# A channel gate over an image that is larger than the on-chip memory: other chunk sizes, and GpSimd beside VectorE

## The chip, the cores and the metric

The kernel runs on one core of a Trainium2 chip. The metric is the device time of one execution in microseconds (us), as the median of several runs; lower is better. Engines are named as in the profile: PE is TensorE, DVE is VectorE, ACT is ScalarE, POOL is GpSimd, SP is the engine whose queue issues nearly all DMA transfers here.

## What is computed

```
H = W = 384; C = 384; k = 1
x: (1, H, W, C) bfloat16, w1d: (1,) bfloat16

g = einsum("bhwc->bc", x) / (H * W)      # mean of each channel
s = sigmoid(g * w1d[0])                  # k = 1: a kernel of one tap
return x * s[:, None, None, :]
```

The whole image has to be summed before the first output value is known. x has 147,456 pixels of 384 channels, 113.25 MB, and the output has as many.

## The kernel before

**Tiles and rows.** The pixels are split over the 128 partitions, 1152 per partition. The program calls one pixel per partition a row: 384 bf16 numbers (768 bytes) in each partition, 98,304 bytes over all. One large tile, the arena, holds 275 rows. Everything is loaded into it, changed in place, and stored from it.

**First phase: sum, and keep what fits.** All 1152 rows are loaded once. TensorE adds each row into a PSUM bank with a matrix of ones (`sum_rows`, one matmul per row, line 242). 784 rows are streamed: summed, overwritten, and read a second time later. The other 368 are kept. Of those, 72 raw rows stay as they are, and the rest sits in groups that are folded. A group of q row quadruples is loaded as 4q rows. `fold` (line 292) spreads the 16 bits of every fourth number over spare exponent bits of the three others, so that q of the 4q rows come free and the next group can be laid over them. There is one group with q = 4 (`FIRST`), eight with q = 8 (`PAIR`; 32 rows each, in two columns of the arena, at 12 and at G0 = 116), and one with q = 6 (`BANKED`) that ScalarE copies into PSUM and brings back later. A fold works in pieces of 16 rows (`PIECE` = 4 rows of each quarter), with scratch rows at T and Y. A vote (`seen`, `verdict`, `again`) has GpSimd redo the kept groups should a number not have the expected exponent; it doesn't with these inputs.

The order of the loads is written out by hand: after the first two groups the streamed rows go in chunks of 52 and of 64 (`EARLY`), then groups and chunks by turns (`BETWEEN`), the last three groups in parts because less of the arena is free, then the raw rows in small loads. On TensorE's queue the sums stand in the order of the loads. With chunks of over 40 rows 16 extra matmuls of a zero tile are put in front (`keep_warm`).

**The turn.** ScalarE makes the sigmoid (`s_bf`, line 451) and copies it into PSUM as well (`s_ps`, line 455).

**Second phase: scale and store.** `scale` (line 464) multiplies rows with the gate in place, on VectorE. Only at the start does GpSimd take three scales of 4 rows (`alongside`), while VectorE reads the gate from PSUM (`s_ps`) instead of SBUF (`s_bf`). `unfold` (line 484) rebuilds a piece of 16 rows in four steps: `fields`, `signs`, `three`, `fourth`. They are tensor_scalar operations on bits (line 276), joins (tensor_tensor, line 282) and scales. Stores (line 474) and the second loads of the streamed rows (line 236) go through SP's queue in order; an instruction at its head that waits holds up all behind it.

**The planner.** The order of the second phase comes from a small model that runs while the program is built (lines 576 to 781). It keeps a clock for VectorE and a list of transfers, and decides at each tick what is scaled, unfolded, stored or loaded next. Its output is an order of instructions, not times: on the chip only semaphores hold an instruction. Its parameters: VectorE prefers landed chunks to unfolding while less than `PENDING` us of transfers are ahead; scaled parts are stored together unless less than `MERGE` us are ahead; a load takes the longest free run of rows, up to `CAP`, if it has `BIG` rows, or less when under `LOW` or `LAST` us are ahead; a landed load is scaled in parts of at most `PART` rows; `DEEP` and `SHORT` say when a load may follow a store.

`Flow` (line 21) records every step with the rows it reads and writes and turns conflicts into semaphore waits. DMA completions use 24 semaphores per queue in turn.

Of the kernel before, what the change touches and what calls it, by code (L numbers as in the profile page):

```python
# [11 lines left out]
class Step:  # L12
    __slots__ = ("eng", "emit", "dma", "lane", "deps", "wanted", "rank", "waits", "know", "i")

    def __init__(self, eng, emit, dma):
        self.eng, self.emit, self.dma = eng, emit, dma
        self.deps, self.wanted, self.rank, self.waits, self.know = [], False, 0, [], None
        self.lane = None


class Flow:
# [12 lines left out]
    def add(self, eng, emit, reads=(), writes=(), dma=False, after=()):  # L34
        s = Step(eng, emit, dma)
        s.i = len(self.steps)
# [31 lines left out]
    def emit(self):  # L68
# [37 lines left out]
        with self.tc.tile_critical():  # L106
            for s in self.steps:
# [3 lines left out]
                for h, v in waits:  # L111
                    eng.wait_ge(h, v)  # L112
                ins = s.emit()
# [14 lines left out]
def kernel(  # L128
# [32 lines left out]
    N_A = 39  # L161
# [186 lines left out]
    folding = False  # L348
    N_WARM = 16

    def stream(n, a):
        load(STREAMED, a, streamed[0], streamed[0] + n)
        if n > 40 and folding:
            keep_warm(N_WARM)
        sum_rows(a, n)
        streamed[0] += n

    def stream_all(where, n=None):
        i = 0
        n = sum(m for _, m in where) if n is None else n  # L360
        while n:
            a, m = where[i % len(where)]
            m = min(n, m)
            stream(m, a)
            n -= m
            i += 1
# [30 lines left out]
    for i, (lo, hi, corner) in enumerate(corners):  # L397
        copy_bank(i, arena[:, SPARE, lo:hi], corner, rows(SPARE, 1), [("corner", i)])

    S1, S2 = [(A, 20)], [(A + 20, N_A - 20)]  # L400

    HIGH = [(A - 48, 48)]
    LOW_COLUMN = [(G0 - 48, 48)]


    take(FIRST)
    fold(0)
    EARLY = [(A - 64 * i, 64) for i in (3, 2, 1)]
    BETWEEN = [
        LOW_COLUMN, HIGH,  # L410
        LOW_COLUMN, [(A, N_A)],
        [(G0 - 24, 24), (A - 24, 24)], (S1, S2),
        (S1, S2), (S1, S2),
    ]
    between = sum(n for b in BETWEEN for w in b for _, n in (w if isinstance(w, list) else [w]))
    first = N_STREAM - between
    stream_all(EARLY[2:], first % 64)
    stream_all(EARLY, first - first % 64)
    folding = True


    for g, where in zip(range(1, BANKED), BETWEEN):
        k1, k2 = of_group(g)
        if isinstance(where, list):
            take(g)
            fold(k1)
            fold(k2)
            stream_all(where)
        else:
            take(g, 0, 12)  # L430
            take(g, 24, 32)
            fold(k1)
            stream_all(where[0])
            take(g, 12, 24)
            fold(k2)
            stream_all(where[1])
# [6 lines left out]
    for a, n in [(U, 8)] + S1 + [(A + 20, 11), (A + 31, 8), (V, 8), (Y + 1, 6), (T + 5, 4), (T + 2, 3), (T, 2)]:  # L443
        take_raw(a, n)
# [24 lines left out]

    def store(chunk, a, lo, hi):  # L470
# [7 lines left out]
    def unfold(k, first):  # L478

        g, lo, p = pieces[k]  # L480
        a, at = first + 3 * lo, first + 3 * GROUPS[g][1] + lo
        w, wc = flat(a, 3 * p), [rows(a + j * p, p) for j in range(3)]
        w0, w1, w2 = (flat(a + j * p, p) for j in range(3))
        ba, ca = Y, Y + PIECE
        u, b, c = flat(at, p), flat(ba, p), flat(ca, p)
        uc, bc, cc = rows(at, p), rows(ba, p), rows(ca, p)
        more = int(k == of_group(BANKED)[-1])

        def fields():
            bits(u, w0, SHR, 4, AND, 0x0780, wc[0], uc)  # L490
            bits(b, w1, SHR, 8, AND, 0x0078, wc[1], bc)
            join(u, u, b, OR, uc + bc, uc)

        def signs():
            bits(c, w2, SHR, 12, AND, 0x0007, wc[2], cc)
            bits(b, w2, SHL, 4, AND, 0x8000, wc[2], bc)
            join(u, u, c, OR, uc + cc, uc)

        def three():
            wall = wc[0] + wc[1] + wc[2]  # L500
            bits(w, w, AND, 0x87FF, OR, 0x3800, wall, wall)
            join(u, u, b, OR, uc + bc, uc)
            scale(a, 3 * p)

        def fourth():

            bits(u, u, XOR, FIX, AND, 0xFFFF, uc, uc)
            scale(at, p + more)

        return [  # L510
            (fields, 2 * TS(p) + TT(p)),
            (signs, 2 * TS(p) + TT(p)),
            (three, TS(3 * p) + TT(p) + TT(3 * p)),
            (fourth, TS(p) + TT(p + more)),
        ]

    def TS(n):
        return 0.15 + 0.1 * n

# [60 lines left out]
    DEEP, SHORT = 6.5, 1.0  # L580
    BANKS_AT = 2
# [81 lines left out]
    def start_group():  # L663
# [26 lines left out]
        for k in of_group(g):  # L690
            turns.extend(step + (None,) for step in unfold(k, a))
        sent, n_rows = 0, 4 * q + (g == BANKED)
        if len(line) >= total - N_SPLIT and q == PAIR:

            f, t, _ = turns[-6]
            sent = 3 * PIECE
            turns[-6] = (f, t, lambda: send(KEPT, a, c_group[g], c_group[g] + sent, part, written))
# [4 lines left out]
    while True:  # L702

        if dve_at <= now:
# [4 lines left out]
            if landed and (ahead < PENDING or not can):  # L709
                chunk, a, lo, n, end = landed.popleft()  # L710
                scale(a, n, s=s_ps if alongside and now else s_bf)
                dve_at = now + TT(n)
# [5 lines left out]
            elif can:  # L718
                f, t, then = turns.popleft()
                f()  # L720
                dve_at = now + t
# [14 lines left out]
        if out_rows == total and not checked:  # L736
            checked = True
            fl.add("POOL", again, reads=["odd_i", "s_bf"], writes=rows(Y, N_OVER), after=written)
# [41 lines left out]
        now += DT  # L780
    fl.stall, fl.total = stall, now
# [33 lines left out]
```

## Time and profile before

| what | value |
|---|---|
| median of 3 runs | 719.91 us |
| lowest, highest | 719.8, 720.5 us |
| the profiled execution: its own time | 720.22 us |
| the profiled execution: span from first to last instruction | 718.4 us |
| moved by the DMA in the span | 303.69 MB |
| of it read and written in HBM | 190.32 MB, 113.25 MB |
| mean granted TensorE clock | 0.665 |

The profile comes from one execution. Its page gives busy time by engine, the span in 40 slices, the DMA queues, the chain of work that ended last, and groups of instructions by line. Other views of the same trace give busy time in chosen stretches, waits, and instructions in order of time. A share of the DMA is the time that packets took, over 16 engines; since records overlap a little, it can be slightly above 1. In rows of groups the shapes are partitions x elements; 384 elements are one row, so 128x1536 are 4 rows and 128x6144 are 16.

### The profile page before, as it was taken

Reading aid. Unit: us, or ns where it says so; the run is one execution under the profiler, and the core shown is the slowest. Engines: PE = TensorE matmul, PEld = TensorE weight load, DVE = VectorE, ACT = ScalarE, POOL = GpSimd, SP = SyncE. Lnnn points to the kernel's source line nnn. Section 1 sums busy time; section 2 is a strip of 40 time slices with the busy share of each in tenths; the row PEclk is TensorE's granted clock in tenths of the full one; section 3 lists DMA queues with packets and bytes.
Section 4 is the critical chain, followed back from the end, with each engine's and each line's share of the span. In section 5 each row is a group of like instructions: output and inputs, shape, how many; then the busy total and the mean of one; then the engine's idle time right before and its main releaser. Section 6 shows DMA issues by size and latency. Waiting matters only on the chain.

```text
span 718.4 us, 2070 instructions
## 1 busy us (share of the span) xinstructions
PE 214.4 (30%) x1202; PEld 0.3 (0%) x3; DVE 494.5 (69%) x474; ACT 116.5 (16%) x97; POOL 9.4 (1%) x7
## 2 busy tenths in 40 slices
PE   4667978989887880000000000000000000000000
PEld 0000000000000000000000000000000000000000
DVE  4600001978998929989998999989999965464430
ACT  3700001666777620001000000000000000000000
POOL 0000000000000004000000000000000000000000
PEclk9898999999999995555555555555555555555555
DMA  9999999999999989999999999999999999999997
GB/s 376 440 438 436 438 435 418 434 435 424 423 430 425 427 332 385 402 432 426 423 427 426 431 433 445 420 437 434 435 426 433 431 431 432 432 443 433 424 432 325
DMA packets 19741, 303.69 MB, mean 423 GB/s; under 512 B 2194, under 2 KB 3346, under 8 KB 6290
## 3 DMA queue, kind: packets, MB, share of 16 engines
q1 hardware_dynamic: 19728, 303.57, 99.1%
q8 instruction: 4, 0.07, 0.0%
q14 instruction: 7, 0.06, 0.0%
q10 hardware_dynamic: 2, 0.00, 0.0%
HBM read 190.32 MB, written 113.25 MB: 423 GB/s over the span
## 4 chain that ended last, share of the span: by engine, by line
DMA 72%; DVE 14%; PE 7%; ACT 2%; SPq 0%; issue 0%; another core or an unknown queue 0%; DVEq 0%
DMA arena<-in_x_dram 49%; DMA out_dram<-arena 23%; DVE arena L464 11%; PE bank L242 7%; ACT arena L313 2%; DVE arena L276 2%; DVE arena L282 1%; SPq L236 0%; SPq L474 0%; ACT s_bf L451 0%; SPq L112 0%; DVEq L112 0%; SPq L810 0%; SPq L106 0%
## 5 line engine op out<-in xcount | busy, mean ns | idle before, releaser
L464 DVE TENSOR_TENSOR arena<-arena,s_bf 128x4608 bf16<-128x4608 bf16 (+8 forms) x95 | 228.0, 2431 | 85.6 <-DMA arena<-in_x_dram 71.6
L242 PE MATMUL bank<-arena,ones 128*128 128x384 bf16 x1151 | 206.0, 343 | 44.9 <-DMA arena<-in_x_dram 44.8
L276 DVE TENSOR_SCALAR arena<-arena 128x1536 uint16<-128x1536 uint16 (+2 forms) x247 | 145.1, 632 | 105.5 <-DMA arena<-in_x_dram 99.5
L282 DVE TENSOR_TENSOR arena<-arena 128x1536 uint16<-128x1536 uint16 (+2 forms) x114 | 121.1, 1063 | 10.4 <-PE bank L242 7.6
L313 ACT ACTIVATE arena<-arena 128x3072 uint16<-128x3072 uint16 (+1 forms) x38 | 102.5, 2696 | 143.7 <-DVE arena L276 143.7
L541 PE MATMUL bank<-odd,ones 128*128 128x1 bf16 x1 | 0.2, 186 | 317.4 <-DVE odd L536 317.4
L388 ACT COPY arena<-bank 128x512 uint32<-128x512 uint32 (+2 forms) x8 | 4.2, 533 | 68.9 <-DMA out_dram<-arena 68.7
L464 POOL TENSOR_TENSOR arena<-arena,s_bf 128x1536 bf16<-128x1536 bf16 x3 | 9.2, 3099 | 268.7 <-ACT bank L455 268.7
L464 DVE TENSOR_TENSOR arena<-arena,bank 128x768 bf16<-128x768 bf16 (+5 forms) x12 | 12.5, 1113 | 0.0
L242 PE MATMUL bank<-s_bf,ones 128*128 128x384 bf16 x48 | 8.3, 326 | 0.0
L313 ACT ACTIVATION_READ_ACCUMULATOR arena<-arena 128x1 f32 x38 | 7.1, 186 | 0.0
L388 ACT COPY bank<-arena 128x512 uint32<-128x512 uint32 (+2 forms) x8 | 3.8, 529 | 0.0
L451 ACT ACTIVATE s_bf<-bank,w_sc 128x384 bf16<-128x384 f32 x1 | 0.6, 580 | 12.5 <-PE bank L242 12.5
L256 PE MATMUL bank<-arena,ones 128*128 128x384 bf16 x1 | 0.5, 480 | 6.9 <-DMA arena<-in_x_dram 6.9
L783 ACT ACT_TABLE_LOAD x1 | 1.3, 1283 | 0.7 <-PEq L799 0.7
L333 DVE MEMSET ones<- 128x128 bf16 x1 | 0.2, 165 | 1.1 <-SPq L106 1.1
L338 PE MATMUL bank<-w_bf,ones 1*128 1x1 bf16 x1 | 0.2, 182 | 2.1 <-DMA w_bf<-in_w1d_dram 2.1
L343 DVE TENSOR_SCALAR w_sc<-bank 128x1 f32<-128x1 f32 x1 | 0.2, 159 | 0.9 <-PE bank L338 0.9
L545 DVE CAST odd_i<-bank 128x1 int32<-128x1 f32 x1 | 0.2, 157 | 0.3 <-PE bank L541 0.3
L541 PEld LDWEIGHTS bank<-odd,ones 128*128 128x128 bf16 x1 | 0.1, 104 | 576.3 <-DVE odd L536 576.3
L455 ACT COPY bank<-s_bf 128x192 uint32<-128x192 uint32 x1 | 0.3, 323 | 0.0
L388 ACT COPY arena<-rest 128x64 uint32<-128x64 uint32 x1 | 0.2, 244 | 0.0
(10 smaller groups left out, 1.4 us busy)
## 6 DMA issues: line engine op xcount, KB each, us to landing
arena<-in_x_dram SPq DMA_DIRECT2D x6, 6144.0 KB, 33.8
arena<-in_x_dram SPq DMA_DIRECT2D x6, 4608.0 KB, 28.7
out_dram<-arena SPq DMA_DIRECT2D x8, 3072.0 KB, 30.8
arena<-in_x_dram SPq DMA_DIRECT2D x7, 3072.0 KB, 29.3
out_dram<-arena SPq DMA_DIRECT2D x3, 4608.0 KB, 43.4
arena<-in_x_dram SPq DMA_DIRECT2D x3, 4512.0 KB, 28.8
out_dram<-arena SPq DMA_DIRECT2D x3, 4512.0 KB, 35.4
out_dram<-arena SPq DMA_DIRECT2D x10, 1248.0 KB, 11.1
```

Of the source, the lines that this page charges most:

```text
L242: return pe.add_instruction(mybir.InstMatmult(name=nc.get_next_instruction_name(), ins=[pe.lower_ap(rhs), pe.lower_ap(ones[:])], outs=[pe. ...
L256: return nc.tensor.matmul(acc, lhsT=ones[:], rhs=arena[:, i, :], start=first, stop=last)
L276: lambda: nc.vector.tensor_scalar(out=dst, in0=src, scalar1=s0, scalar2=s1, op0=op0, op1=op1),
L282: "DVE", lambda: nc.vector.tensor_tensor(out=dst, in0=a, in1=b, op=op), reads=reads, writes=writes
L313: lambda: nc.scalar.activation(out=y, in_=y, func=ACTF.Copy, accum_out=seen[:, 2 * k + i : 2 * k + i + 1]),
L333: fl.add("DVE", lambda: nc.vector.memset(ones[:], 1.0), writes=["ones"])
L388: "ACT", lambda: nc.scalar.copy(dst.bitcast(u32), src.bitcast(u32)), reads=reads, writes=writes
L451: lambda: nc.scalar.activation(out=s_bf[:], in_=acc, func=ACTF.Sigmoid, scale=w_sc[:, 0:1]),
L455: "ACT", lambda: nc.scalar.copy(s_ps.bitcast(u32), s_bf[:].bitcast(u32)), reads=["s_bf"], writes=["bank0"]
L464: lambda: vec.tensor_tensor(out=v, in0=v, in1=s[:, None, :].to_broadcast([P, n, C]), op=Op.mult),
L541: lambda: nc.tensor.matmul(votes, lhsT=ones[:], rhs=odd[:], start=True, stop=True),
L783: nc.scalar.preload_act_table(ACTF.Sigmoid)
```

## The change

It has four parts. (1) The order of the first phase is a list (`PLAN`): S loads a chunk of streamed rows at a place (with a third number, only so many of its rows are summed at once, the others after the next load's instructions), K takes a group or a part of it, F folds. The chunks have other sizes, 19 to 80 rows; the rows streamed, kept and folded are the same ones in number. (2) `unfold` takes a group of 32 rows in one go: the operations work on two blocks of 4 rows at a stride, and the scale of the three rebuilt quarters is a step of its own. (3) `scale_both` gives n // 5 rows of a chunk of 10 or more to GpSimd, from when `alongside` is done until no group is left to unfold; VectorE then reads the gate from PSUM. (4) The planner's parameters change at 70, 200 and 300 us of its clock; loads may then have up to 96 rows, and are scaled in parts of up to 32. Besides, GpSimd waits in front of `again` by an instruction of its own (`block`). With all this the program issues 113 transfers in place of 137.

The diff, cut to its core:

```diff
+                if s.block and hold:
+                    eng.wait_ge(*hold)
+                    hold = None
...
-    def stream(n, a):
+    def stream(a, n, at_once=None):
         load(STREAMED, a, streamed[0], streamed[0] + n)
-        if n > 40 and folding:
+        if n > 40 and streamed[0] > N_STREAM // 2:
             keep_warm(N_WARM)
-        sum_rows(a, n)
+        m = n if at_once is None else at_once
+        sum_rows(a, m)
         streamed[0] += n
+        return a + m, n - m
...
+    PLAN = [
+        ("S", 156, 52), ("S", 92, 62), ("S", 26, 66), ("S", 160, 60), ("S", 108, 48), ("S", 28, 64, 6),
+        ("S", 156, 80), ("K", 1), ("F", 1), ("S", 68, 48), ("K", 2), ("F", 2), ("S", 172, 52), ("K", 3), ("F", 3),
+        ("S", 68, 48), ("K", 4), ("S", 220, 39, 16), ("K", 5), ("F", 4), ("F", 5), ("S", 92, 24, 19), ("S", 196, 24),
+        ("K", 6), ("F", 6), ("S", 220, 20), ("K", 7, 24, 32), ("S", 240, 19), ("K", 7, 0, 12), ("F", 7, 0),
+        ("S", 220, 20), ("K", 7, 12, 24), ("S", 240, 19), ("K", 8, 0, 12), ("S", 220, 20), ("K", 8, 24, 32),
+        ("F", 7, 1), ("F", 8, 0), ("K", 8, 12, 24), ("S", 240, 19), ("F", 8, 1),
+    ]
+    due_rows = (A, 0)
+    for kind, a, *more in PLAN:
+        if kind == "S":
+            sum_rows(*due_rows)
+            due_rows = stream(a, *more)
+        elif kind == "K":
+            take(a, *more)
+            sum_rows(*due_rows)
+            due_rows = (A, 0)
         else:
+            for k in of_group(a):
+                if not more or k == of_group(a)[more[0]]:
+                    fold(k)
...
+    def share(n):
+        return n // 5 if beside[0] and n >= 10 else 0
+
+    def scale_both(a, n):
+        m = share(n)
+        before = [s for s in fl.steps[-40:] if s.eng == "DVE"][-1:]
+        scale(a, n - m, s=s_ps if beside[0] else s_bf)
+        if m:
+            scale(a + n - m, m, "POOL", after=before)
...
+    def unfold_rows(a, at, p, n, more):
+        blocks = arena[:, a : a + 3 * n, :].bitcast(u16).rearrange("q (b j r) c -> q b j (r c)", j=3, r=p)
+        w0, w1, w2 = (blocks[:, :, j, :] for j in range(3))
...
         def fields():
+            bits(us, w0, SHR, 4, AND, 0x0780, wc, uc)
+            bits(ys, w1, SHR, 8, AND, 0x0078, wc, yc)
+            join(u, u, y, OR, uc + yc, uc)
 
         def signs():
+            bits(ys, w2, SHR, 12, AND, 0x0007, wc, yc)
+            join(u, u, y, OR, uc + yc, uc)
+            bits(ys, w2, SHL, 4, AND, 0x8000, wc, yc)
 
         def three():
+            bits(w, w, AND, 0x87FF, OR, 0x3800, wc, wc)
+            join(u, u, y, OR, uc + yc, uc)
+
+        def threefold():
+            scale_both(a, 3 * n)
 
         def fourth():
             bits(u, u, XOR, FIX, AND, 0xFFFF, uc, uc)
+            scale(at, n + more, s=s_ps if beside[0] else s_bf)
...
     while True:
+        if now > 70:
+            BIG, CAP, PART, LOW, LAST = 32, 48, 20, 2, 1
+            MERGE, DEEP, SHORT, PENDING = 2, 2, 0.5, 40
+        if now > 200:
+            BIG, CAP, PART, LOW, LAST = 88, 96, 32, 6, 3
+            MERGE, DEEP, SHORT, PENDING = 3, 8, 2, 24
+        if now > 300:
+            BIG, CAP, PART, LOW, LAST = 40, 96, 32, 5, 2
+            MERGE, DEEP, SHORT, PENDING = 2, 20, 0.5, 18
...
+                beside[0] = BESIDE and not alongside and bool(line or turns)
+                if beside[0]:
+                    scale_both(a, n)
+                else:
+                    scale(a, n, s=s_ps if alongside and now else s_bf)
+                dve_at = now + SC(n)
```

114 lines of the change are left out of this document (39 added, 75 removed).

## The prediction, made before the result was known

> **What bounds the kernel now.** I read the page's head first, then the engines' busy time in five stretches, then what the SP queue waits for. In the page the DMA rows decide:
>
> ```profile
> span 718.4 us, 2070 instructions
> PE 214.4 (30%) x1202; PEld 0.3 (0%) x3; DVE 494.5 (69%) x474; ACT 116.5 (16%) x97; POOL 9.4 (1%) x7
> ...
> DMA packets 19741, 303.69 MB, mean 423 GB/s; under 512 B 2194, under 2 KB 3346, under 8 KB 6290
> ...
> q1 hardware_dynamic: 19728, 303.57, 99.1%
> ```
>
> The 16 DMA engines are busy for 99.1% of the span, 711.9 us. The diff changes no size of the arena, no group and no number of kept rows, so the 303.57 MB stay. The packets also tell what one transfer is: 2194 are under 512 B, and 137 transfers times 16 is 2192, so each transfer ends with one small packet on each engine; the other 17,536 of the queue are 137 x 128, one per partition and transfer. The next rows give, for stretches from the span's start, each engine's busy us, then DMA share and GB/s.
>
> ```profile
> core 0: us, PE busy (x) PEld busy (x) DVE busy (x) ACT busy (x) POOL busy (x), PEclk, DMA share, GB/s
> 0.00:4.00 4.00, 0.18 (x1) 0.10 (x1) 0.53 (x3) 1.28 (x1) 0.20 (x4) 1.00 0.50 163
> 4.00:264.00 260.00, 209.89 (x1177) 0.10 (x1) 137.80 (x190) 109.87 (x85) 0.00 (x0) 0.93 1.00 429
> 264.00:272.00 8.00, 4.12 (x24) 0.00 (x0) 3.23 (x8) 0.90 (x2) 2.83 (x1) 0.99 0.56 212
> 272.00:712.00 440.00, 0.19 (x1) 0.10 (x1) 352.94 (x275) 4.40 (x9) 6.38 (x3) 0.50 1.01 429
> 712.00:718.40 6.40, 0.00 (x0) 0.00 (x0) 0.00 (x0) 0.00 (x0) 0.00 (x0) 0.50 0.30 127
> 280.00:585.00 305.00, 0.00 (x0) 0.00 (x0) 292.58 (x250) 4.40 (x9) 0.00 (x0) 0.50 1.01 429
> 254.00:260.00 6.00, 4.16 (x26) 0.00 (x0) 1.52 (x2) 1.65 (x2) 0.00 (x0) 1.00 0.94 355
> ```
>
> The DMA is idle in three places only: 2.0 us at the start, 3.5 at the turn from summing to scaling (8 us at 0.56), 4.5 at the end (6.4 us at 0.30). Between them the share is 1.00 or 1.01 (records overlap a little, so 1.01 means no gap). VectorE is 96% busy from 280 to 585 (292.58 of 305), which looks like the bound and isn't: with VectorE this full the DMA still has no gap. The SP queue agrees:
>
> ```profile
> SPq L474 <- DVE arena L464: 272.1, 49, 25.5
> SPq L236 <- PE bank L242: 168.3, 18, 32.2
> SPq L236 <- DMA out_dram<-arena: 123.2, 25, 16.6
> ```
>
> SP waits 272.1 us for scales, but while it waits earlier transfers are still in flight. So a faster VectorE earns nothing by itself; a transfer less earns its fixed cost.
>
> **The change part by part.** *Transfers.* What one costs shows when the same bytes go in differently many. The rows are for 40:120 (64-row loads), 300:400, 440:700; the columns are packets, MB and share.
>
> ```profile
> DMA packets 879, 34.92 MB, mean 436 GB/s; under 512 B 96, under 2 KB 96, under 8 KB 96
> ...
> q1 hardware_dynamic: 877, 34.89, 101.0%
> ```
> ```profile
> DMA packets 4651, 42.81 MB, mean 428 GB/s; under 512 B 514, under 2 KB 514, under 8 KB 1410
> ...
> q1 hardware_dynamic: 4649, 42.79, 101.3%
> ```
> ```profile
> DMA packets 4254, 112.47 MB, mean 433 GB/s; under 512 B 474, under 2 KB 474, under 8 KB 474
> ...
> q1 hardware_dynamic: 4252, 112.45, 100.4%
> ```
>
> 64-row loads (6.29 MB each) move 34.89 MB in 80.8 us of engine time, 0.4318 MB/us. At that rate 42.79 MB take 99.1 us; they took 101.3, 2.2 more, for 514/16 = 32.1 transfers where 64-row ones would be 6.8: 2.2/25.3 = 0.087 us each. For 440:700: 260.4 against 261.0, 0.6 for 11.7 more, 0.05. For the whole span: 703.0 against 711.9, 8.9 for 137 - 48.3 = 88.7, 0.10. I take 0.08, between the two late stretches and nearer to 300:400, because that is where transfers vanish: the plan of the first phase counts 43 loads where there were 45, so 22 of the 24 fall into the second, whose planner keeps its old parameters for its first 70 us. Sum: 24 x 0.08 = **1.9 us**, ends 1.2 and 2.4.
>
> *The new order of the first phase.* Group 1 is loaded after 473 rows (25 + 16 + 432 streamed) where it came after 477 (25 + 16 + 436). Ahead of it stands an 80-row chunk in place of a 64-row one, and TensorE sums in order, so group 1's sums come later:
>
> ```profile
> 53.71 10.57 PE bank L242 x64
> ```
>
> 10.57 us for 64 is 0.165 a row: 16 rows more, 2.6 us later. VectorE's fold then waits, but groups 2 to 4 follow 80 to 84 rows apart, 18 to 19 us of DMA, against some 15 us of folding (137.80 us of VectorE in 4:264 for 19 pieces, two to a group), and it catches up. The last scratch loads wait for the last fold in both kernels; in 254:260 the share is 0.94, so at most 0.4 us is to be won. The closest reload, 20 rows at 220, comes 39 rows (8.9 us of DMA) after the load whose rows it takes, and their sums take 3.3. The raw loads that end the phase are unchanged, and so is the idle 3.5 us. I cost this at nothing; if the fold ends late, the phase ends late by as much.
>
> *VectorE.* Rows by operation and shape, count, busy us, mean ns:
>
> ```profile
> L276 DVE TENSOR_SCALAR arena<-arena 128x1536 uint16<-128x1536 uint16 x199 | 100.9, 553 | 4.6 <-ACT arena L313 3.0
> L282 DVE TENSOR_TENSOR arena<-arena 128x1536 uint16<-128x1536 uint16 x91 | 86.7, 953 | 1.3
> L464 DVE TENSOR_TENSOR arena<-arena,s_bf 128x6144 bf16<-128x6144 bf16 x22 | 72.9, 3353 | 47.8 <-DMA arena<-in_x_dram 47.8
> L464 DVE TENSOR_TENSOR arena<-arena,s_bf 128x4608 bf16<-128x4608 bf16 x24 | 60.9, 2550 | 1.3 <-DMA arena<-in_x_dram 1.3
> L464 DVE TENSOR_TENSOR arena<-arena,s_bf 128x4992 bf16<-128x4992 bf16 x13 | 35.5, 2753 | 2.1 <-DMA arena<-in_x_dram 2.1
> L282 DVE TENSOR_TENSOR arena<-arena 128x3072 uint16<-128x3072 uint16 x18 | 31.6, 1758 | 9.0 <-PE bank L242 7.6
> L276 DVE TENSOR_SCALAR arena<-arena 128x4608 uint16<-128x4608 uint16 x18 | 24.3, 1351 | 0.0
> L276 DVE TENSOR_SCALAR arena<-arena 128x3072 uint16<-128x3072 uint16 x18 | 17.3, 960 | 100.8 <-DMA arena<-in_x_dram 99.5
> L464 DVE TENSOR_TENSOR arena<-arena,s_bf 128x1536 bf16<-128x1536 bf16 x18 | 17.2, 958 | 0.6
> L464 POOL TENSOR_TENSOR arena<-arena,s_bf 128x1536 bf16<-128x1536 bf16 x3 | 9.2, 3099 | 268.7 <-ACT bank L455 268.7
> L464 DVE TENSOR_TENSOR arena<-arena,bank 128x4992 bf16<-128x4992 bf16 x2 | 5.5, 2744 | 0.0
> ```
>
> A piece of 16 rows takes 5 x 0.553 + 1.351 + 3 x 0.953 + 2.550 + 0.958 = 10.5 us, a group 21.0. In one go: 5 x 0.960 + 3 x 1.758 + 1.758, a tensor_scalar over 24 rows (by the step from 8 to 12 rows, 2.55) and a scale of 20 rows on VectorE (by the step from 12 to 16, 4.16): 18.5. Eight groups: 19 us less. Of the streamed rows some 530 are scaled before 585 in parts of 13 to 20, about a sixth of them now on GpSimd: 90 rows x 0.209 = 19 us less. So 38 us of VectorE's 292.58 go. By the DMA's share they were hidden already: **nothing**. The blocked views (two runs of 4 rows at a stride) of tensor_scalar are in no row; if they ran as slowly as the join, four operations per group would cost 0.8 us more, 26 us, covered by the 38.
>
> *GpSimd.* It takes a fifth of the rows: 3.099 us for 4, 0.775 a row, against 0.209 for each of VectorE's four: 16 rows 3.35 beside 3.10. Stores now wait for both engines, and SP holds loads behind such a store; in parts of 10 to 32 rows GpSimd ends first by 0.2 us or more, so nothing comes late. The final check on GpSimd's queue stands behind all its scales, as chunks are shared only while groups are left. VectorE reads the scale from PSUM beside GpSimd, which costs it nothing (4992 elements: 2744 against 2753). The trace has the two side by side:
>
> ```profile
> 269.13 12.46 DVE L464 TENSOR_TENSOR arena<-arena,bank 128x768 bf16<-128x768 bf16 x12
> ...
> 269.17 9.21 POOL L464 TENSOR_TENSOR arena<-arena,s_bf 128x1536 bf16<-128x1536 bf16 x3 [268.73 <-ACT bank L455]
> ```
>
> The Trainium skill, SBUF — State Buffer, "SBUF: two separate sides", speaks against sharing: VectorE and GpSimd share a port pair as an exclusive lock, the loser blocks for the whole instruction, when VectorE has two SBUF inputs or runs in a 2-port mode. By the same rule the PSUM operand avoids the lock, and the rows just quoted agree with that; what stands behind GpSimd's operation (the unfold's bit operations) would block if GpSimd ran late.
>
> *Sum.* The profiled execution took 720.22 (span 718.4 and 1.8 around it), the median of the three runs is 719.91: 719.9 - 1.9 = **718.0**.
>
> **The rivals.** *No measurable change:* the fixed cost is at its low end of 0.05, or half of the gain is lost to gaps under 1 us at two or three places, since stores of 40 and more rows leave fewer pieces to choose from: 719 to 720.5. For it: the gain is a quarter of a per cent. Against: no gap in 440 us now.
>
> *More gain:* 0.10 a transfer, the 0.4 us before the turn, and 1 to 2 of the 4.5 us at the end: 715.5.
>
> *Slower, the DMA runs dry behind a late large chunk.* The end of before:
>
> ```profile
> 665.96 32.67 SPq L474 DMA_DIRECT2D out_dram<-arena  x3
> 691.64 6.63 DVE L464 TENSOR_TENSOR arena<-arena,s_bf 128x6144 bf16<-128x6144 bf16 x2 [19.17 <-DMA arena<-in_x_dram]
> ```
>
> The last load lands at 691.6, VectorE scales for 6.63 us, and stores already queued keep the DMA at work beside it. With parts of 32 rows the first store can follow after 32 rows at the earliest, 3.353 + 4 x 0.803 = 6.6 us, and some 1 us from issue to first bytes; a 96-row chunk stored whole, after 19.7. It decides when less than that is queued at a landing: one such place costs up to 7.6 and gives 725.6, a whole chunk up to 20.7, 738.7. Against: three chunks of 90 fit into 275 rows, and VectorE needs 0.209 a row where the DMA needs 0.228 twice.
>
> *Slower, the engines exclude each other:* 122 rows x 0.775 = 95 us of GpSimd are added to VectorE's path and 38 taken away; 57 more on an engine with 12 us to spare in that stretch gives about 763. The quoted stretch speaks against it.
>
> *Slower, long rows are cut:* no transfer in the trace has over 64 rows (48 KiB per partition, one packet). If 96 rows were cut row by row, small packets show the price (284:290, mostly 2-row stores):
>
> ```profile
> q1 hardware_dynamic: 243, 2.32, 106.1%
> ```
>
> 2.32 MB took 6.37 us where 5.37 would do, 1.19 times; on 21.9 us that is 4.1 per transfer, some four of them 16, so 734. [...]
>
> **How the numbers follow.** Forecast (717.5 to 718.7) 0.50, no measurable change 0.17, more gain 0.09, dry DMA 0.17, exclusion 0.03, cut rows 0.04. A measurement of this kernel can tell about 0.2% (1.4 us) from no change. Of the forecast 0.42 lies below 718.5: faster 0.42 + 0.09 = 0.51. Same 0.08 + 0.17 = 0.25. Slower 0.17 + 0.03 + 0.04 = 0.24. The range reaches from the larger gain, 715.5, into the dry case at one partly covered place, 723.5; what lies beyond is under 0.2.
>
> **What would show it.** Right: 303.57 MB in 113 x 16 = 1808 small packets; engine time about 710; DMA share 1.00 or above from 4 us to the turn and from there to the last few us; VectorE visibly below 96% from 280 to 585 without a gain from it; GpSimd's scales near 0.775 us a row and VectorE's beside them unslowed. Wrong: a stretch with share under 0.97, above all after 600; bit operations longer than their 0.55 and 0.96 us; more than 128 large packets per transfer; a turn later than 264 to 272.

## The result and the profile after

| | before | after |
|---|---|---|
| median (lowest to highest) of 7 runs each on one chip | 719.80 us (718.83 to 721.02) | 722.08 us (720.95 to 722.97) |
| ratio, 95% interval | | 1.0030 [1.0019, 1.0040] |
| the profiled execution: its own time, span | 720.22, 718.4 us | 721.53, 719.8 us |
| first store issued (the turn) | 269.16 us | 268.32 us |
| from there to the end of the span | 449.2 us | 451.5 us |
| transfers | 137 | 113 |

The kernel became slower by 0.3%, where 1.9 us of gain were forecast. The head of the page after, to be held against the first fence of the prediction:

```profile
span 719.8 us, 2010 instructions
PE 214.4 (30%) x1202; PEld 0.3 (0%) x3; DVE 467.9 (65%) x369; ACT 116.5 (16%) x97; POOL 92.9 (13%) x41
...
DMA packets 17052, 303.68 MB, mean 422 GB/s; under 512 B 1810, under 2 KB 2962, under 8 KB 5650
...
q1 hardware_dynamic: 17040, 303.57, 98.9%
```

The bytes stayed, the small packets fell to 1808 (113 x 16; two of the 1810 are of other queues), VectorE lost 26.6 us of work and GpSimd got 83.5. But 98.9% of 719.8 us is 711.9 us of DMA time, what it was before: the time of 24 transfers was given back somewhere. The turn even comes 0.8 us earlier, so the loss lies in the second phase (from the turn, where the first store is issued, to the end of the span). Busy time by stretch (columns as in the prediction), after and then before:

```profile
540.00:552.00 12.00, 0.00 (x0) 0.00 (x0) 11.02 (x2) 0.00 (x0) 0.00 (x0) 0.50 0.98 397
552.00:600.00 48.00, 0.00 (x0) 0.00 (x0) 27.17 (x5) 0.00 (x0) 0.00 (x0) 0.50 1.00 419
600.00:620.00 20.00, 0.00 (x0) 0.00 (x0) 9.63 (x2) 0.00 (x0) 0.00 (x0) 0.50 1.01 433
```
```profile
540.00:552.00 12.00, 0.00 (x0) 0.00 (x0) 11.96 (x11) 0.00 (x0) 0.00 (x0) 0.50 1.00 419
552.00:600.00 48.00, 0.19 (x1) 0.10 (x1) 41.22 (x35) 0.00 (x0) 0.00 (x0) 0.50 1.00 430
600.00:620.00 20.00, 0.00 (x0) 0.00 (x0) 2.12 (x1) 0.00 (x0) 0.00 (x0) 0.50 1.00 430
```

In 540:552 the rate falls to 397 GB/s. In 552:600 the share is back at 1.00 and the rate isn't: the same bytes take longer. At before's rates the missing bytes would take 12 x 22/419 + 48 x 11/430 = 0.6 + 1.2 = 1.9 us (rounded), most of the 2.3 by which the second phase grew. What SP issues there, and what its loads waited for between 505 and 562 (us in total, times, longest):

```profile
511.04 0.39 SPq L240 DMA_DIRECT2D arena<-in_x_dram  x1
522.19 10.23 SPq L469 DMA_DIRECT2D out_dram<-arena  x2
548.27 0.39 SPq L240 DMA_DIRECT2D arena<-in_x_dram  x1
559.71 0.38 SPq L469 DMA_DIRECT2D out_dram<-arena  x1
```
```profile
SPq L240 <- DMA out_dram<-arena: 33.9, 2, 18.1
```

The sizes and the times from issue to landing, in the stretch 505:565:

```profile
arena<-in_x_dram SPq DMA_DIRECT2D x1, 9216.0 KB, 27.3
...
out_dram<-arena SPq DMA_DIRECT2D x1, 3072.0 KB, 26.1
out_dram<-arena SPq DMA_DIRECT2D x1, 1536.0 KB, 19.8
```

The load at 548.27 has 96 rows (9216 KB). Part of the place it takes belongs to the store of 32 rows issued at 522.2, which lands 26.1 us later, at 548.3: the load is issued the moment that store has landed. Behind it in the DMA's queue lie only the 16 rows (1536 KB, 3.7 us of transfer) of the other store. By the packet records the 16 DMA engines end that store up to 3.3 us apart, and an engine that finishes early has nothing until the load's first packets, 1.0 us after its issue: some 0.7 us per engine without a packet. I call this the **dry place**. The store after it is issued at 559.71, too late to help.

### The profile page after: what moved, and what is told of

The parts are those of the page before. It is cut to its first block, busy times and chain, and to the rows that moved or that the text cites. A ratio compares the mean times of both kernels' runs of the same rounds, so it can differ in the third digit from the quotient of the medians.

```text
span 719.8 us, 2010 instructions
## 1 busy us (share of the span) xinstructions
PE 214.4 (30%) x1202; PEld 0.3 (0%) x3; DVE 467.9 (65%) x369; ACT 116.5 (16%) x97; POOL 92.9 (13%) x41
## 2 busy tenths in 40 slices
DMA packets 17052, 303.68 MB, mean 422 GB/s; under 512 B 1810, under 2 KB 2962, under 8 KB 5650
## 3 DMA queue, kind: packets, MB, share of 16 engines
q1 hardware_dynamic: 17040, 303.57, 98.9%
## 4 chain that ended last, share of the span: by engine, by line
DMA 54%; DVE 25%; PE 16%; ACT 1%; issue 1%; SPq 0%; DVEq 0%
DMA arena<-in_x_dram 36%; DMA out_dram<-arena 18%; DVE arena L446 16%; PE bank L246 16%; DVE arena L280 5%; DVE arena L286 3%; ACT arena L317 1%; SPq L240 0%; ACT s_bf L433 0%; SPq L113 0%; SPq L839 0%; DVEq L113 0%; SPq L107 0%
## 5 line engine op out<-in xcount | busy, mean ns | idle before, releaser
L280 DVE TENSOR_SCALAR arena<-arena 128x1536 uint16<-128x1536 uint16 (+2 forms) x199 | 140.4, 750 | 117.8 <-DMA arena<-in_x_dram 99.3
L446 POOL TENSOR_TENSOR arena<-arena,s_bf 128x1536 bf16<-128x1536 bf16 (+2 forms) x37 | 92.6, 2508 | 437.2 <-ACT bank L437 267.9
L446 DVE TENSOR_TENSOR arena<-arena,s_bf 128x12288 bf16<-128x12288 bf16 (+7 forms) x15 | 83.2, 5594 | 89.2 <-DMA arena<-in_x_dram 79.1
L446 DVE TENSOR_TENSOR arena<-arena,bank 128x3072 bf16<-128x3072 bf16 (+12 forms) x59 | 131.4, 2270 | 4.7 <-DMA arena<-in_x_dram 4.2
L286 DVE TENSOR_TENSOR arena<-arena 128x3072 uint16<-128x3072 uint16 (+2 forms) x90 | 117.6, 1306 | 12.8 <-PE bank L246 9.9
```

The lines of the kernel that those rows point to most:

```text
L280: lambda: nc.vector.tensor_scalar(out=dst, in0=src, scalar1=s0, scalar2=s1, op0=op0, op1=op1),
L286: "DVE", lambda: nc.vector.tensor_tensor(out=dst, in0=a, in1=b, op=op), reads=reads, writes=writes
L446: lambda: vec.tensor_tensor(out=v, in0=v, in1=s[:, None, :].to_broadcast([P, n, C]), op=Op.mult),
```

## Experiments

**Theories.** The main one: the late planner parameters (from 200 us of its clock) ask for 88 free rows and up to 96; a planner that holds out for 88 lets smaller free runs lie, and a load comes to wait for a store's landing with little queued behind: the dry place and the slow packets after it are the loss. Its rivals for the loss: rows of over 64 KiB per partition cost something; the first phase's order does; GpSimd beside VectorE does; or a transfer simply costs less than I took.

All runs. "Second phase" is, in the profiled execution, from the first store issued to the end of the span.

| run | transfers | median (lowest to highest, n) us | before beside it | ratio [95%] | second phase us |
|---|---|---|---|---|---|
| after | 113 | 722.08 (720.95 to 722.97, 7) | 719.80 | 1.0030 [1.0019, 1.0040] | 451.5 |
| before_new_first_phase | 135 | 719.95 (719.37 to 722.91, 12) | 719.63 | 1.0011 [1.0000, 1.0021] | 449.6 |
| after_long_split | 119 | 721.47 (720.61 to 723.33, 7) | 719.63 | 1.0030 [1.0019, 1.0040] | 451.3 |
| after_cap_80 | 115 | 722.79 (720.43 to 723.24, 7) | 719.63 | 1.0037 [1.0024, 1.0049] | 451.0 |
| after_old_parameters | 130 | 720.05 (719.35 to 721.29, 11) | 719.63 | 1.0008 [0.9999, 1.0016] | 448.9 |
| after_load_earlier | 113 | 722.22 (721.57 to 723.62, 6) | 719.51 | 1.0035 [1.0022, 1.0048] | 451.1 |
| before_forced_dry | 137 | 725.47 (724.59 to 726.03, 5) | 719.51 | 1.0074 [1.0061, 1.0087] | 454.8 |
| before_quarters | 272 | 726.54 (725.55 to 727.62, 5) | 719.51 | 1.0090 [1.0076, 1.0105] | 453.8 |
| after_vector_alone | 113 | 727.77 (726.61 to 728.36, 4) | 719.51 | 1.0104 [1.0089, 1.0119] | 457.4 |
| after_big_40 | 115 | 721.24 (719.94 to 722.17, 7) | 719.71 | 1.0020 [1.0009, 1.0032] | 449.6 |
| old_parameters_vector_alone | 130 | 720.51 (719.76 to 722.04, 11) | 719.71 | 1.0015 [1.0006, 1.0024] | 449.8 |
| after_late_old_parameters | 123 | 720.09 (718.99 to 721.74, 11) | 719.71 | 1.0009 [1.0000, 1.0018] | 448.5 |
| before_cap_96 | 133 | 719.49 (719.09 to 720.04, 11) | 719.53 | 0.9999 [0.9990, 1.0007] | 448.9 |
| after_big_40_cap_48 | 121 | 720.67 (719.32 to 722.36, 12) | 719.53 | 1.0017 [1.0007, 1.0027] | 449.1 |
| after_big_40_look_1 | 115 | 719.10 (1) | 719.53 | | 448.5 |
| after_big_40_look_2 | 115 | 722.07 (1) | 719.53 | | 449.4 |
| old_first_phase_big_40 | 117 | 720.77 (719.41 to 722.96, 12) | 719.69 | 1.0017 [1.0007, 1.0027] | 448.9 |
| old_first_phase_late_old | 125 | 720.76 (719.86 to 722.30, 11) | 719.69 | 1.0015 [1.0005, 1.0024] | 450.2 |

**The first phase alone.** Before, with the new `PLAN` of loads, sums and folds and nothing else of the change (the loop's head stands here for the whole edit).

```diff
-    for g, where in zip(range(1, BANKED), BETWEEN):
...
+    for kind, a, *more in PLAN:
```

> The kernel before with the new order of the first phase alone (135 transfers). In the profile of the changed kernel the first store is issued at 268.32 us where it was 269.16. Theory 1 (the whole loss lies in the second phase, the first phase gains): 0.6 to 1.0 us faster than before, 719.0, first store near 268.3. Rival (the 0.8 us is scatter between executions, or the new order of loads is itself slower): same as before within 0.3 us or slower, first store at 269 or later.

0.3 us in the medians, an interval that begins at no change: no part of the loss that can be told. The turn comes at 268.27. The loss isn't here.

**Long transfers issued as two.** After, where every transfer of over 85 rows is issued as two halves; order and waits stay.

```diff
-            known.append(store(chunk, a, lo, lo + n))
+            known.extend(store_parts(chunk, a, lo, lo + n))
...
+                m = n // 2 if n > 85 else n
-                load(STREAMED, a, todo, todo + n)
+                load(STREAMED, a, todo, todo + m)
+                if m < n:
+                    load(STREAMED, a + m, todo + m, todo + n)
```

> The changed kernel in the same order, but each transfer of over 85 rows is issued as two transfers of half the rows (119 transfers). In the changed kernel's trace 113 transfers left 119 x 128 large packets, so six transfers of over 64 KiB per partition went as two packets per partition, and many of the packets of the second halves took 0.3 to 1.9 us too long (about 2.2 us of the 16 engines' time in 550 to 615). Theory 1 (the cut inside one transfer costs that): 1.5 to 2.5 us faster than the changed kernel, about 720, and no slow 48-row packets. Rival 2 (the slow packets come with the row order or the place in memory, or by chance, not with the cut): within 0.5 us of the changed kernel, about 722.3, slow packets still there.

**Loads of at most 80 rows.**

```diff
-            BIG, CAP, PART, LOW, LAST = 88, 96, 32, 6, 3
+            BIG, CAP, PART, LOW, LAST = 80, 80, 32, 6, 3
...
-            BIG, CAP, PART, LOW, LAST = 40, 96, 32, 5, 2
+            BIG, CAP, PART, LOW, LAST = 40, 80, 32, 5, 2
```

> The changed kernel with loads of at most 80 rows late (115 transfers, none over 64 KiB per partition). Theory 1 (long cut rows): 720 to 720.5, slow packets gone after 540. Rival 2 (a gap of the DMA where the late coarse stores end, at 547 us 0.7 us in the trace of the changed kernel): the gap stays and the time is above 721.5.

Both are as slow as after, so the length of a row isn't it. The dry place is still in both (0.5 to 0.6 us per engine without a packet); the stretch 540:600 of the split one and of the other, where 600:700 runs at 436 and 433 GB/s:

```profile
540.00:600.00 60.00, 0.00 (x0) 0.00 (x0) 32.21 (x5) 0.00 (x0) 0.00 (x0) 0.50 0.99 417
```
```profile
540.00:600.00 60.00, 0.00 (x0) 0.00 (x0) 32.63 (x7) 0.00 (x0) 0.00 (x0) 0.50 1.01 423
```

**The old parameters throughout.** After without the three blocks that change the planner's parameters.

```diff
-        if now > 70: ...
-        if now > 200: ...
-        if now > 300: ...
```

> The changed kernel without the three new sets of planner parameters (130 transfers): new first phase, whole-group unfold and GpSimd stay. Theory 1 (the loss comes from the late large transfers alone): 718.5 to 719.3, faster than before by the first phase's 0.8 and 7 transfers less at 0.05 to 0.08 each. Rival 3 (GpSimd beside VectorE, or the unfold in one go, costs the time): 721.5 to 722.5.

2.0 us of the loss go with the parameters; the rest of the change stands at 720.05, 0.4 above before and not told apart from it.

**The waiting load put behind another one.** At 548 a run of 47 free rows was there already, which the planner didn't take since it held out for 88. After, with that 47-row load moved ahead of the 96-row load on SP's queue, so that it covers the wait.

```diff
+    sp = [s for s in fl.steps if s.dma and s.eng == "SP"]
+    fl.steps.remove(sp[106])
+    fl.steps.insert(fl.steps.index(sp[104]), sp[106])
```

> The changed kernel with one instruction moved: the load of 47 rows to row 220, which stands behind the 96-row load to row 116 and the store after it on SP's queue, is put ahead of that 96-row load. Same 113 transfers of the same sizes. In the changed kernel's trace the 96-row load waits on SP until the 32-row store into its rows has landed (548.27 us), only a 16-row store is queued then, the DMA runs dry (idle 0.7 us a engine within 542 to 552), and packets of the next 30 us take 2.0 us longer in sum. Theory 2 (the dry place, and the slow packets that follow the common restart, are the loss): 2 to 3 us faster than the changed kernel, 719 to 720, no idle stretch and no slow packets after 540. Theory 1 (long transfers of over 85 rows as such): within 0.5 us of the changed kernel, slow packets stay.

The total didn't move (722.22), so the expected gain wasn't had. In the trace the place at 548 is gone and another one has come at 602.

```profile
540.00:552.00 12.00, 0.00 (x0) 0.00 (x0) 10.53 (x2) 0.00 (x0) 0.00 (x0) 0.50 1.04 446
552.00:600.00 48.00, 0.00 (x0) 0.00 (x0) 23.34 (x5) 0.00 (x0) 0.00 (x0) 0.50 1.00 433
602.00:612.00 10.00, 0.00 (x0) 0.00 (x0) 10.00 (x3) 0.00 (x0) 0.00 (x0) 0.50 0.74 316
612.00:650.00 38.00, 0.00 (x0) 0.00 (x0) 1.86 (x1) 0.00 (x0) 0.00 (x0) 0.50 1.02 419
```

446 and 433 GB/s where after had 397 and 419; then 10 us at a share of 0.74, while VectorE works all of the 10 and the store at SP's head waits for its scale until 604.7, and 38 us at 419. As I read it, the load taken early is missing as cover later. So moving one load can't tell the price of the place, but it shows the pattern a second time: idle engines, then slow packets.

**A dry place made in before.** Before, where one late load waits for the landing of the store ahead of it (a wait more, no work more).

```diff
+    sp = [s for s in fl.steps if s.dma and s.eng == "SP"]
+    sp[122].deps.append(sp[121])
```

> The kernel before with one wait added: the 48-row load to row 148 also waits for the 48-row store issued just ahead of it, so that the DMA must run dry once, in an order without any transfer over 64 rows. Theory 2: the idle place costs about 3 us (receipt, issue, and the spread of the 16 engines) and slow packets after the restart add 1 to 2: 723.5 to 725. Rival (a dry place costs its idle time alone, and the slow packets of the changed kernel came with its long transfers): 722 to 723 and no slow packets behind it.

It costs 5.96 us, and the trace accounts for it. Before, then with the wait:

```profile
572.00:584.00 12.00, 0.00 (x0) 0.00 (x0) 11.93 (x13) 0.00 (x0) 0.00 (x0) 0.50 1.01 436
584.00:602.00 18.00, 0.19 (x1) 0.10 (x1) 11.35 (x8) 0.00 (x0) 0.00 (x0) 0.50 0.98 424
```
```profile
572.00:584.00 12.00, 0.00 (x0) 0.00 (x0) 11.90 (x14) 0.00 (x0) 0.00 (x0) 0.50 0.65 255
584.00:602.00 18.00, 0.18 (x1) 0.10 (x1) 6.91 (x6) 0.00 (x0) 0.00 (x0) 0.50 1.03 418
602.00:650.00 48.00, 0.00 (x0) 0.00 (x0) 23.07 (x8) 0.00 (x0) 0.00 (x0) 0.50 1.00 430
```

Idle time is 4.1 us per engine by the packet records (by the share of 572:584 it would be 12 x 0.35 = 4.2), and in 572:650 the packets take some 2 us more than the same bytes do in before, about half of it in 584:602: 6.1 against 5.96 measured. This dry place thus cost its idle time and about 2 us more in slow packets, and nothing later gave it back.

**More transfers, nothing else.** Before, with each transfer of 32 and more rows issued as four.

```diff
+        if hi - lo >= 32:
+            for e, f in quarters(hi - lo):
+                load(chunk, a + e, lo + e, lo + f)
+            return
...
```

> The kernel before with each transfer of 32 and more rows issued as four, 272 transfers in place of 137, the same bytes in the same order. It measures the disputed price of a transfer. By the prediction's 0.08 us: 135 x 0.08 = 10.8 us, 730.4. By 0.05, the low end: 6.8 us, 726.4. Theory 3 (records overlap, so what a transfer costs in records is mostly not time): under 4 us, below 723.6.

7.03 us for 135 transfers: **0.052 us each**. At that price the saving of 24 is 1.25 us, not 1.9.

**GpSimd's fifth given to VectorE.** After in the same order on SP's queue; VectorE scales all rows.

```diff
-        scale(a, n - m, s=s_ps if beside[0] else s_bf)
-        if m:
-            scale(a + n - m, m, "POOL", after=before)
+        scale(a, n, s=s_ps if beside[0] else s_bf)
```

> The changed kernel in the same order of SP's queue, but VectorE scales the fifth that went to GpSimd as well. Theory 2: GpSimd has no part in the loss; VectorE gets some 25 us more work in the unfolding stretch and comes later, so the same time within 1 us of the changed kernel or slower, 722 to 727. Rival (GpSimd beside VectorE costs time by contention, at the port or in memory): faster than the changed kernel by over 1 us.

5.7 us slower than after. The stretches 310:440 and 440:552 without GpSimd, then 310:440 of after:

```profile
310.00:440.00 130.00, 0.00 (x0) 0.00 (x0) 128.75 (x79) 4.40 (x9) 0.00 (x0) 0.50 1.01 411
440.00:552.00 112.00, 0.19 (x1) 0.10 (x1) 102.85 (x58) 0.00 (x0) 0.00 (x0) 0.50 1.00 430
```
```profile
310.00:440.00 130.00, 0.00 (x0) 0.00 (x0) 125.42 (x84) 4.40 (x9) 43.32 (x18) 0.50 1.01 431
```

In 310:440 VectorE is busy 128.75 of 130 us and the rate is 411 GB/s at the same share of 1.01: not a gap but slower packets, and 130 x 20/431 = 6.0 us, as much as was lost. That VectorE's lateness makes the packets slow is likely and not shown. GpSimd is no cause of the loss; in this order it is needed.

**No GpSimd at the old parameters.** The first phase and the unfold in one go, without the sharing.

```diff
-    BESIDE = True
+    BESIDE = False
-        if now > 70: ...
-        if now > 200: ...
-        if now > 300: ...
```

> The changed kernel with the planner's old parameters and without GpSimd (its order is planned for VectorE alone): what stays of the change is the new first phase and the unfold in one go, 130 transfers. By the prediction's step that a faster VectorE earns nothing: the same as with GpSimd at the old parameters, 720.05, within 0.6 us, with VectorE busier by some 17 us from 280 to 585. Rival (the fifth on GpSimd is worth time even there): over 1 us slower.

720.51 against 720.05 with GpSimd, the intervals overlap: at the old parameters the sharing earns nothing that can be told, which fits VectorE's time being hidden there.

**88 rows to 40.** After, where the planner between 200 and 300 us of its clock takes loads from 40 free rows on.

```diff
-            BIG, CAP, PART, LOW, LAST = 88, 96, 32, 6, 3
+            BIG, CAP, PART, LOW, LAST = 40, 96, 32, 6, 3
```

> The changed kernel with one number changed: between 200 and 300 us of the planner's clock a load needs 40 free rows to be issued at once, not 88 (115 transfers, of which some still have 92 to 96 rows). By the order on SP's queue no load then waits for the last but one queued store: where the changed kernel has a 16-row store left as cover, every load after 540 has over 25 rows of work queued ahead. Theory 2 (one dry place, 0.7 us idle and 2 us of slow packets after it, is the whole loss): 718.4 to 719.4, that is 0.2 to 1.2 faster than before (22 transfers at the 0.05 us that the quartered transfers showed), no idle and no slow packets after 540. Theory 1 (long transfers as such are slow): 721.5 to 722.5, slow packets at the 92 to 96-row transfers.

Two transfers more, and the dry place is gone:

```profile
540.00:600.00 60.00, 0.19 (x1) 0.10 (x1) 25.31 (x10) 0.00 (x0) 0.47 (x1) 0.50 1.00 428
600.00:700.00 100.00, 0.00 (x0) 0.00 (x0) 47.22 (x8) 0.00 (x0) 0.00 (x0) 0.50 1.00 434
```

The second phase falls from 451.5 to 449.6, before's 449.2 within 0.4. But the median, 721.24, fell by 0.8 us only and its interval overlaps that of after. The spans of the same runs tell more, since they leave out the time around the span: 718.5 (717.5 to 720.1) where after has 720.1 (719.2 to 720.9), 1.6 us less.

**Old parameters from 200 us on.** After, where only the middle block of parameters (70 to 200 us) is kept.

```diff
-            BIG, CAP, PART, LOW, LAST = 88, 96, 32, 6, 3
-            MERGE, DEEP, SHORT, PENDING = 3, 8, 2, 24
-        if now > 300: ...
+            BIG, CAP, PART, LOW, LAST = 32, 48, 16, 9.0, 4.0
+            MERGE, DEEP, SHORT, PENDING = 12.0, 6.5, 1.0, 24.0
```

> The changed kernel with the parameters for 70 to 200 us of the planner's clock kept and the old ones from 200 us on (123 transfers). Theory 2: the loss sits in the late part alone, so 718.8 to 719.8, no slow packets after 540. Rival (the middle parameters, 20-row parts and little queued ahead, lose too): above 721.

720.09, ratio 1.0009 [1.0000, 1.0018], which doesn't reach after's [1.0019, 1.0040]: the late parameters carry most of the loss, and the other parts of the change with 14 of the 24 saved transfers stand at no change or 0.2% above.

**Long loads in before.**

```diff
-    BIG, CAP, PART, LOW, LAST = 32, 48, 16, 9.0, 4.0
+    BIG, CAP, PART, LOW, LAST = 32, 96, 16, 9.0, 4.0
```

> The kernel before with one number changed: loads of up to 96 rows in place of 48 (133 transfers; one load and one store of 92 rows and two of each of 64). By the order of SP's queue no transfer runs out of cover. Theory 1 (long transfers as such cost time, also without a dry place): 720.5 to 721.5 where before has 719.6. Theory 2 (only a dry queue costs): 719.2 to 719.8.

719.49 with transfers of up to 92 rows: long ones cost nothing as such, nor do four transfers less earn what can be measured.

**40 and at most 48 rows.** After with both late `BIG` at 40 and both late `CAP` at 48.

```diff
-            BIG, CAP, PART, LOW, LAST = 88, 96, 32, 6, 3
+            BIG, CAP, PART, LOW, LAST = 40, 48, 32, 6, 3
...
-            BIG, CAP, PART, LOW, LAST = 40, 96, 32, 5, 2
+            BIG, CAP, PART, LOW, LAST = 40, 48, 32, 5, 2
```

> The changed kernel with 40 rows enough for a load and 48 the most of one in the late part (121 transfers): neither a dry place nor a transfer of over 48 rows after the first phase. Theory 1 and 2 alike: 718.8 to 719.8. Rival (what the version with 40 and 96 still loses comes from the middle part, from GpSimd or from the unfold in one go): 720.5 to 721.5.

720.67, not told apart from after_big_40.

**Two more executions of the kernel with 40** (no further edit), since its runs scatter more than before's.

> Another execution of the version with 40 in place of 88. Its median was 721.24 while its profiled execution took 720.0, one of its fastest. Theory 2: an execution of 721 and more has a dry stretch or slow packets that the other one doesn't have, at the place with the least cover. Rival (the time is lost evenly): share and rate in every stretch alike, only the span longer.

> As the look before it: a second execution, to see whether a slower one loses its time in the same stretch.

They came out at 719.10 and 722.07, the two ends of the scatter. Of the 2.97 us between them 1.06 lie ahead of the turn (268.59 and 269.65), 0.9 in the second phase (448.5 and 449.4), and 1.0 outside the span (2.05 and 3.06 us around it). No single place carries it.

**The old first phase with each of the two.** The first phase of before put back into after_big_40 and into after_late_old_parameters.

```diff
-    for kind, a, *more in PLAN:
...
+    for g, where in zip(range(1, BANKED), BETWEEN):
```

> The version with 40 in place of 88, with the first phase of before put back (117 transfers): whole-group unfold, GpSimd and the new late parameters without the dry place. In the traces so far the first store is issued between 268.3 and 269.7 us with the new first phase and between 268.6 and 269.2 with the old, and the medians of all versions with the new one spread upwards. If the new first phase makes what is left of the loss: 718.6 to 719.5, below the version with the new one (721.24), and no more scatter than before. If the second phase with 92 to 96-row chunks makes it: 720.5 to 721.5.

> The version with the old parameters from 200 us on, with the first phase of before put back (125 transfers). If the new first phase makes what is left of the loss: 718.6 to 719.4, a little faster than before by 12 transfers at 0.05. If GpSimd, the unfold in one go or the middle parameters make it: 720 or more.

720.77 and 720.76, where the new first phase had 721.24 and 720.09: the old one made one a little faster and the other a little slower, so the small rest of the loss isn't the first phase either. The second one's interval, [1.0005, 1.0024], does reach after's; by the spans it stands at 718.6, 1.5 us below after.

**What is settled and what is open.** The three kernels that were slowed (forced wait, quarters, VectorE alone) aside, the four traces with a dry place (after, split, cap 80, load earlier) have a second phase of 451.0 to 451.5 us, and before and the eleven others have 448.5 to 450.2. The middles of the two groups lie some 2 us apart, and undoing the late parameters takes 2.0 us off the median. The spans of all runs divide the same way: medians of 719.7 to 721.0 us for the four, 717.8 to 718.6 for the changed kernel's versions without a dry place, 717.6 to 717.9 for before. Shown, then: the late parameters, and the 88 rows in them above all, lose the time, and the trace places it at the dry place. How much of the 2 us the place alone costs is read from the traces; no run takes out that place and nothing else. Open, too: the versions of the changed kernel without the place still stand 0.4 to 1.5 us above before in the median (0.0 to 0.9 by the spans), where 7 to 22 transfers less at 0.052 us should have gained 0.4 to 1.1. About 0.25 us of that lies outside the span (the median of time less span is 1.80 us for before and about 2.05 for the versions that share with GpSimd and have no dry place); the remainder was not placed. No version was measurably faster than before; before_cap_96 comes closest with 719.49 against 719.53.

## Why the prediction was wrong, point by point

**The step that failed: "Slower, the DMA runs dry behind a late large chunk", with the argument against it, "three chunks of 90 fit into 275 rows".** The mechanism was there, as a rival; I had looked for it at the last landing and only between a load and its scales, and given it 0.17. It occurred at a load that waits for a store to land, in the middle of the second phase. Room for three chunks doesn't help when the planner insists on one free run of 88: the run it got was made of rows under a store still on its way. I read the diff's `BIG` as a size and not as a rule of when a load may be issued. The prediction's own sign for it, "a stretch with share under 0.97, above all after 600", was also too coarse: 540:552 stood at 0.98, since the loss is more in the packets after than in the gap, and since the share counts a packet whole in the stretch where it starts. In the sum a term of about +2 us was missing. With it and with 1.25 us for the transfers (next point) the sum gives 719.9 - 1.25 + 2 = 720.65; the 1.4 us from there to 722.08 are the rest that stays open.

**Transfers, "24 x 0.08 = 1.9 us": mis-sized.** Measured 0.052, so 1.25 us. I had sized it from shares of the DMA; where records overlap (shares of 1.01 and more) these count some time twice, which would explain an overstatement. The end at 0.05, from the stretch of large transfers, was right. The sign for the gain, engine time of about 710 us, failed: it was 711.9, with the slow packets in it.

**"I cost this at nothing", the first phase: right in the sum, short in the wait.** TensorE's sums for fold 1 come later, as said; VectorE after, and the wait of the same join before:

```profile
119.49 1.90 DVE L280 TENSOR_SCALAR arena<-arena 128x3072 uint16<-128x3072 uint16 x3 [86.83 <-DMA arena<-in_x_dram]
128.45 1.76 DVE L286 TENSOR_TENSOR arena<-arena 128x3072 uint16<-128x3072 uint16 x1 [7.06 <-PE bank L246]
```
```profile
124.66 1.76 DVE L282 TENSOR_TENSOR arena<-arena 128x3072 uint16<-128x3072 uint16 x1 [2.49 <-PE bank L242]
```

It waits 7.06 us where before waited 2.49, 4.6 more and not 2.6; the folds catch up, and the turn comes at 268.32. The old first phase has its turn between 268.41 and 269.16 in five traces (quarters, with other transfers, aside), so the 0.8 us can be scatter. The stretch before the turn shows 0.3 of the 0.4 us that were to be won, 0.99 for 0.94:

```profile
254.00:260.00 6.00, 4.11 (x27) 0.00 (x0) 3.79 (x6) 2.86 (x2) 0.00 (x0) 1.00 0.99 416
```

**VectorE and GpSimd: right.** Groups of instructions by shape:

```profile
L286 DVE TENSOR_TENSOR arena<-arena 128x3072 uint16<-128x3072 uint16 x42 | 73.8, 1757 | 11.8 <-PE bank L246 9.9
L280 DVE TENSOR_SCALAR arena<-arena 128x3072 uint16<-128x3072 uint16 x58 | 54.8, 956 | 110.8 <-DMA arena<-in_x_dram 97.4 <-DMA out_dram<-arena 11.3 <-ACT arena L317 0.2
L446 DVE TENSOR_TENSOR arena<-arena,bank 128x7680 bf16<-128x7680 bf16 x8 | 33.2, 4145 | 0.0
```
```profile
L446 POOL TENSOR_TENSOR arena<-arena,s_bf 128x1536 bf16<-128x1536 bf16 x19 | 58.8, 3101 | 391.5 <-ACT bank L437 267.9 <-DVE arena L286 101.1 <-DVE arena L280 10.2
```

The two-block views run at 0.956 us, and the scale of 20 rows takes 4.145 where 4.16 was worked out, beside GpSimd at 3.101 for 4 rows. No exclusion: with a PSUM operand VectorE isn't held up. This agrees with the Trainium skill (SBUF — State Buffer, "SBUF: two separate sides"), which names two SBUF inputs or a 2-port mode for VectorE's side of the lock. GpSimd got 106 rows more (118 in its 37 scales, less 12 before) and not 122. The durations of VectorE's operations, added up as the prediction added them (count times mean), fell by 37.1 us where 38 were forecast; the busy time, which counts the overlap of consecutive records once, fell by 26.6. It earned nothing, as forecast; after_vector_alone shows what the prediction didn't see, that this order needs GpSimd.

**"Long rows are cut": rightly given little.** The 17,040 packets less 1808 small ones are 119 x 128 for 113 transfers: the six of over 64 KiB per partition go as two packets per partition each. After_long_split (721.47 against 722.08) and before_cap_96 (719.49 against 719.53) show no price for them that can be told.

## What to carry to other kernels

Where the DMA is the bound and has no gap, a transfer less earns some 0.05 us, too little to show in the time of any version here, and larger ones can lose 2 us or more at a single place: a larger transfer needs a larger free run, so it is issued later and waits for more. Before raising a minimum size, follow each load that would wait for a store's landing and count what is still queued behind that store; some 4 us of transfer was not enough here. A loss of this kind hardly shows in the busy share: read the rate (GB/s) of the stretch and of the 50 us after it.

## What the runs showed of the hardware that was not expected

**Slow packets after an idle stretch.** In the three traces read for it, the 18 to 48 us behind the place where the DMA ran dry went at a share of 1.00 or more and some 3% below the usual 430 GB/s: 552:600 after (419 GB/s), 584:602 with the forced wait (418), 612:650 with the load moved (419). The stretch after the turn, where the DMA has also been idle, is slow in both kernels, but small packets have a part in that: 560 of the 1534 packets of after in it are under 8 KB. After, then before:

```profile
280.00:310.00 30.00, 0.00 (x0) 0.00 (x0) 28.74 (x18) 0.00 (x0) 9.66 (x5) 0.50 1.01 408
```
```profile
280.00:310.00 30.00, 0.00 (x0) 0.00 (x0) 29.52 (x26) 0.00 (x0) 0.00 (x0) 0.50 1.01 406
```

That it comes from the 16 engines starting again in step is only a thought; nothing here tells it apart from other reasons. Nor does it take an idle stretch: 310:440 of after_vector_alone, with VectorE busy throughout, ran at 411 GB/s.

**The 16 engines drift.** They end the 16-row store before the dry place up to 3.3 us apart, so a queue that holds one small store is empty on some engines while others still work.
